# Decayed linear attention and a mixture of experts: state kept per whole block of 128 tokens instead of per half block

## The chip, the cores and the metric

The kernel runs on one core of a Trainium2 chip. A core has five engines that run their own instruction streams and meet through semaphores: TensorE (PE in the rows; PEld is its loading of weights), VectorE (DVE), ScalarE (ACT), GpSimd (POOL) and SyncE (SP), which here issues nearly all transfers. The metric is the time of one execution on the device in microseconds (us), less is better. An x in a row is a count.

## What is computed

```python
def _attn_ref(q, k, v, alpha):          # (4, 8, 768, 48) each
    state = np.zeros((B, H, D, D))
    for t in range(S):
        state = alpha[:, :, t, :, None] * state + np.einsum('bhd,bhe->bhde', k[:, :, t], v[:, :, t])
        y[:, :, t] = np.einsum('bhd,bhde->bhe', q[:, :, t], state)

def _moe_ref(x, w_skip, w_gate, w1, w2):  # x: (3072, 384), 8 experts, F = 1024
    do_compute = x @ w_skip > 0
    xc = x[do_compute]; logits = xc @ w_gate; e_idx = argmax(logits)
    gate_w = softmax(logits)[e_idx]
    h = relu(xc[e_idx == e] @ w1[e]);  y = gate_w * (h @ w2[e])
    out[do_compute] = xc + y              # the other rows stay x
```

## The kernel before, in words

The sequence of each batch is cut into six chunks of 128 tokens. Two batches are worked alternately, so there are 24 tiles (i = 0 to 23), each with all eight heads of 128 tokens; heads stand in four pairs p, the two heads of a pair on partitions 0 to 47 and 64 to 111 (r = 0, 1). A loop in `static_path` (line 829) runs one step per tile. The instructions of a step are written by hand for several tiles at once, and each engine runs them in the order in which that loop writes them, so the order of the calls is the schedule.

What the calls do for tile i:

- `load` (201): the transfers of decay factors, keys and queries (one tile `qka`) and of the values (`vt`), issued by SyncE five tiles ahead.
- `decay` part 0 and 1 (211): VectorE's running products from the front (`pfx`, 216) and from the back (`sfx`, 224); GpSimd multiplies the queries (220) and keys (226) by them.
- `scores` (229) and `causal` (240): keys times queries for each half of the block (64 keys by 64 queries) into `ps_s`, which VectorE then copies under the causal mask into `st`.
- `turn_k` (244): the keys transposed on TensorE, copied by ScalarE into `kt`.
- `outer` (256): keys times values, added into the state in PSUM (`ps_v`), once per half; after the first half ScalarE copies the half-way state (`half`, 272). `carry` (274) multiplies the state by the decay of the block on VectorE, and `keep` (280) copies it into `state` on ScalarE.
- `inter` (295): queries times state, the first 64 queries with `state`, the other 64 with `half`. `intra` (306): masked scores times values, in two calls. All of it adds up in `ps_y`; `turn_y` (327, its copy is line 330) takes it to SBUF as `xt`.
- `rows` (333), `row_copy` (343), `logits` (348), `store` (353): the output rows and the nine gate logits. `rows` writes into the same PSUM tile `ps_s` as the scores, and the scores of the next tile wait until VectorE has read the logits.

Beside this the loop routes finished tiles in groups of six: `rank` and `place` find slots, `one_hot` (421, line 424 in the rows, GpSimd) builds a 128 by 256 matrix for each tile, and `table` (431, line 436) multiplies with it on TensorE. For the first two groups two one-hot matrices are built per step in three steps (i = 10 to 12 and 16 to 18) and `table` uses them one step later. The weights of the first expert are loaded and split during the loop too. After the loop a tail routes the last tiles, and then eight experts follow (`up` 590, `down` 612).

## Time and profile before

| | |
|---|---|
| median of three runs | 323.0 us (322.78 to 326.44) |
| the profiled execution | 324.42 us, of it the span of the trace 322.6 us |
| busy share of the span | PE 85%, DVE 59%, POOL 59%, ACT 48% |
| TensorE instructions | 4920 matmuls, 4920 weight loads |
| granted TensorE clock, mean | 0.901 of full speed |
| stages in the trace | attention loop to about 158 us, tail to 168.5 us, experts to the end |

Times in the rows of the trace count from the start of the span. The granted clock has two levels, 1.2 and 2.4 GHz; 1.00 in a stretch means 2.4 GHz throughout, 0.50 means 1.2 GHz throughout. A matmul row that says 64*48 64x64 uses 64 rows and 48 columns of the array; TensorE runs several such small ones side by side. In single precision every matmul of the source is two instructions on TensorE, a transpose one. "issue" as a releaser means that an engine waited for nothing that the profile shows.

### The profile page before, as it was taken

How to read it: one execution, taken by the hardware profiler on the slowest of the kernel's cores; microseconds unless marked ns; L12 is line 12 of the kernel's file. 1: busy time of each engine (PE TensorE's matmuls, PEld its weight loads, DVE VectorE, ACT ScalarE, POOL GpSimd, SP SyncE). 2: the span in 40 equal slices, each digit the busy share in tenths (PEclk: the TensorE clock that was granted, in tenths of full speed). 3: DMA queues.
4: the chain of work that ended last, by engine and by line, in shares of the span. 5: the costliest groups of instructions: out<-in, count | busy, mean ns of one | idle time of the engine just before them, and what ended most of it. 6: DMA issues, size and time to landing. Idle time of an engine off the chain costs nothing.

```text
span 322.6 us, 11454 instructions
## 1 busy us (share of the span) xinstructions
PE 273.5 (85%) x4920; PEld 256.9 (80%) x4920; DVE 189.7 (59%) x367; ACT 153.5 (48%) x318; POOL 189.3 (59%) x208
## 2 busy tenths in 40 slices
PE   1997777876888788859789699999999799999991
PEld 1786766866777687759689599999999799999991
DVE  6877677475667566745446516547293576466640
ACT  3145334243335243443415636878685976455510
POOL 4555744445767458672794856737567476755521
PEclk9999799598768779795589689999999999999998
DMA  7997686676657657743502269349498599742000
GB/s 258 410 329 244 213 287 218 194 217 243 208 188 242 208 178 214 225 154 100 203 26 73 80 176 309 106 166 401 139 335 279 185 395 346 261 161 79 15 18 28
DMA packets 25850, 65.44 MB, mean 203 GB/s; under 512 B 3765, under 2 KB 10831, under 8 KB 25792
## 3 DMA queue, kind: packets, MB, share of 16 engines
q1 hardware_dynamic: 23616, 59.58, 55.1%
q0 software_dynamic: 2176, 5.05, 4.7%
q8 instruction: 40, 0.66, 0.8%
q14 instruction: 18, 0.15, 0.1%
HBM read 56.99 MB, written 8.85 MB: 204 GB/s over the span
## 4 chain that ended last, share of the span: by engine, by line
PE 54%; issue 11%; DMA 10%; DVE 8%; ACT 7%; POOL 7%; SPq 1%; POOLq 0%; DVEq 0%; ACTq 0%
PE ps_o L619 14%; PE ps_h L603 13%; PE ps_y L292 7%; PE ps_s L340 5%; DMA raw<-in_w_dram 4%; PE ps_v L266 4%; PE ps_s L237 3%; ACT over L572 3%; PE ps_k L250 3%; POOL hot L424 3%; DVE sfx L224 3%; DMA alpha<-in_nat_dram 3%; ACT x L345 2%; DMA qka<-in_qka_dram 2%; PE ps_g L436 2%
## 5 line engine op out<-in xcount | busy, mean ns | idle before, releaser
L226 POOL TENSOR_TENSOR qka<-qka,sfx 128x512 f32<-128x512 f32 x23 | 29.4, 1277 | 32.2 <-DVE sfx L224 29.2
L619 PE MATMUL ps_o<-w2h,hh 128*112 128x384 f32 (+1 forms) x128 | 44.7, 349 | 0.0
L619 PE MATMUL ps_o<-w2l,hh 128*112 128x384 f32 (+1 forms) x128 | 44.0, 344 | 0.0
L619 PE MATMUL ps_o<-w2h,hl 128*112 128x384 f32 (+1 forms) x128 | 43.7, 341 | 0.0
L220 POOL TENSOR_TENSOR qka<-qka,pfx 128x512 f32<-128x512 f32 x24 | 26.3, 1094 | 23.9 <-PE ps_k L250 8.4
L266 PE MATMUL ps_v<-vt,kt 64*64 64x48 f32 x704 | 36.1, 250 | 4.7 <-issue 4.0
L292 PE MATMUL ps_y<-st,vt 64*48 64x64 f32 x768 | 36.1, 257 | 3.9 <-issue 3.9
L252 ACT COPY kt<-ps_k 128x512 f32<-128x512 f32 x24 | 14.1, 586 | 53.1 <-PE ps_k L250 53.1
L539 POOL TENSOR_TENSOR w2l<-raw,w2h 128x512 fp32r<-128x512 f32 x18 | 24.3, 1351 | 24.6 <-ACT w2h L535 24.6
L266 PEld LDWEIGHTS ps_v<-vt,kt 64*64 64x64 f32 x704 | 32.3, 168 | 5.7 <-issue 4.6
L603 PE MATMUL ps_h<-xh,w1h 128*128 128x240 f32 x192 | 32.8, 277 | 4.0 <-DVE hl L608 2.8
L539 POOL TENSOR_TENSOR w1l<-raw,w1h 128x512 fp32r<-128x512 f32 x24 | 31.6, 1318 | 6.8 <-ACT w1h L535 6.6
L608 DVE SCALAR_TENSOR_TENSOR hl<-ps_h,hh 128x480 fp32r<-128x480 f32 x32 | 20.8, 650 | 22.3 <-ACT hh L607 22.2
L624 POOL DMA_INDIRECT out_dram<-o,ids x16 | 19.0, 1186 | 24.1 <-DVE o L622 23.0
L607 ACT ACTIVATE hh<-ps_h 128x480 fp32r<-128x480 f32 x32 | 18.3, 571 | 31.0 <-PE ps_h L603 27.0
L603 PE MATMUL ps_h<-xh,w1l 128*128 128x240 f32 x192 | 32.4, 275 | 0.0
L603 PE MATMUL ps_h<-xl,w1h 128*128 128x240 f32 x192 | 31.7, 274 | 0.0
L224 DVE TENSOR_TENSOR_SCAN sfx<-qka,ps_c 128x525 f32<-128x525 f32 x24 | 29.9, 1248 | 2.6 <-POOL qka L220 0.5
L216 DVE TENSOR_TENSOR_SCAN pfx<-qka,ps_c 128x527 f32<-128x527 f32 x24 | 29.8, 1241 | 2.6 <-DMA qka<-in_qka_dram 2.6
L292 PEld LDWEIGHTS ps_y<-st,vt 64*48 64x48 f32 x768 | 27.7, 146 | 4.4 <-issue 4.4
L237 PE MATMUL ps_s<-qka 64*64 64x64 f32 x768 | 23.0, 270 | 9.5 <-DVE qka L226 7.1
L603 PEld LDWEIGHTS ps_h<-xh,w1h 128*128 128x128 f32 x192 | 27.3, 190 | 4.6 <-DVE hl L608 3.1
(138 smaller groups left out, 628.3 us busy)
## 6 DMA issues: line engine op xcount, KB each, us to landing
raw<-in_w_dram SPq DMA_DIRECT2D x64, 384.0 KB, 5.4
qka<-in_qka_dram SPq DMA_DIRECT2D x22, 775.5 KB, 4.7
vt<-in_v_dram SPq DMA_DIRECT2D x24, 192.0 KB, 4.7
out_dram<-x SPq DMA_DIRECT2D x24, 192.0 KB, 2.6
alpha<-in_nat_dram SPq DMA_DIRECT2D x8, 576.0 KB, 4.1
out_dram<-xr SPq DMA_DIRECT2D x6, 192.0 KB
qka<-in_qka_dram SPq DMA_DIRECT2D x4, 256.0 KB
qka<-in_qka_dram SPq DMA_DIRECT2D x2, 263.5 KB
```

Source lines behind the costliest of these rows:

```text
L216: nc.vector.tensor_tensor_scan(pfx[:, 0:DEC], dec, self.floor.to_broadcast([P, DEC]), FLOOR, ALU.mult, ALU.max)
L220: nc.gpsimd.tensor_tensor(w["qh"], w["qh"], pfx.rearrange("p (a w) -> p a w", w=SEG)[:, :, 1:P + 1], ALU.mult)
L224: nc.vector.tensor_tensor_scan(sfx[:, 2:DEC][:, ::-1], dec[:, 2:DEC][:, ::-1], self.floor.to_broadcast([P, DEC - 2]), FLOOR, ALU.mult, ALU ...
L226: (eng or nc.gpsimd).tensor_tensor(w["kh"], w["kh"], sfx.rearrange("p (a w) -> p a w", w=SEG)[:, :, 2:P + 2], ALU.mult)
L237: self.nc.tensor.matmul(self.ps[t, r, p * HP:(p + 1) * HP], lhsT=kh[a, p, t], rhs=qh[a, p, t], start=True, stop=True, skip_group_check=True)
L266: ins = self.nc.tensor.matmul(pv[a, p, :], lhsT=w["kt"][t, p, a], rhs=w["v"][t, h * D:(h + 1) * D], start=(i % (G * C) == s == p == 0), st ...
L292: return self.nc.tensor.matmul(self.py[HP * c:HP * c + D, p % 2, o:o + HP], lhsT=lhsT, rhs=rhs, start=first, stop=True, skip_group_check=True)
L539: eng.tensor_tensor(lo[:, s], raw[:, s], hi[:, s].bitcast(F32), ALU.subtract)
L603: nc.tensor.matmul(ps[:, u, :], lhsT=a[:, k, f * P:(f + 1) * P], rhs=b[:, k, :], start=(n == 0), stop=(n == len(order) - 1))
L608: nc.vector.scalar_tensor_tensor(out=hl, in0=ps, scalar=0.0, in1=hh.bitcast(F32), op0=ALU.max, op1=ALU.subtract)
L619: nc.tensor.matmul(ps[:r], lhsT=a[:, f, js], rhs=b[:, f, :], start=(n == 0), stop=(n == 3 * FT - 1))
L624: ins = nc.gpsimd.indirect_dma_start(out=self.out[:, :], out_offset=bass.IndirectOffsetOnAxis(ap=self.ids[:r, j, e:e + 1].bitcast(U32), ax ...
```

## The change

In the loop, each tile's state is kept once per block of 128 tokens and no longer half-way. To make up for the missing half state, the scores of the first 64 keys are taken against all 128 queries (the other 64 keys still against their own 64 queries); the block between (first keys, last queries), which needs no mask, is copied by ScalarE in a new function `cross`. `inter` takes all 128 queries against the old state in one instruction, `outer` takes all 128 tokens at once, and `rows` takes both heads of a pair at once into a bank of its own (`ps_g`). The routing's small products move from `ps_g` into `ps_v`. The transfers of a tile are four instead of two, each issued behind a named matmul, six tiles ahead. One one-hot matrix is built per step in steps 10 to 21. The order of the step is new.

The core of the diff:

```diff
-RW = D + E + 1
+RW = 2 * D + E + 1
...
-    def load(self, i):
-        for s in (slice(0, DEC), slice(KO, QO), slice(QO, QW)) if i < NF else (slice(0, QW),):
-            nc.sync.dma_start(out=t[:, s], in_=self.qka[i, :, s])
-        nc.sync.dma_start(out=vt, in_=self.v[i])
+    def load(self, i, part=None, behind=None):
+        if part == 3:
+            ins = nc.sync.dma_start(out=self.work[i]["v"], in_=self.v[i])
+        else:
+            s = (slice(0, DEC), slice(KO, QO), slice(QO, QW))[part]
+            ins = nc.sync.dma_start(out=self.qkab[i % NQ][:, s], in_=self.qka[i, :, s])
+        if behind:
+            self.follow(ins.ins, behind)
...
     def scores(self, i):
-                    self.nc.tensor.matmul(self.ps[t, r, p * HP:(p + 1) * HP], lhsT=kh[a, p, t], rhs=qh[a, p, t],
-                                          start=True, stop=True, skip_group_check=True)
+                    o = p * P
+                    ins = self.nc.tensor.matmul(self.ps[t, r, o:o + (HP if s else P)], lhsT=kh[a, p, t],
+                                                rhs=qh[a, p, s * HP:], start=True, stop=True, skip_group_check=True)
...
+    def cross(self, i):
+        ps = self.ps.rearrange("k r (a q) -> k r a q", q=P)
+        self.nc.scalar.copy(out=self.work[i]["st"][:HP, :, :, HP:], in_=ps[:HP, :, :, HP:])
...
-    def outer(self, i, s):
+    def outer(self, i):
...
-                ins = self.nc.tensor.matmul(pv[a, p, :], lhsT=w["kt"][t, p, a], rhs=w["v"][t, h * D:(h + 1) * D],
-                                            start=(i % (G * C) == s == p == 0), stop=True, skip_group_check=True)
-        if s == 0:
-            self.nc.scalar.copy(out=w["half"], in_=pv)
+                self.nc.tensor.matmul(pv[a, p, :], lhsT=w["kt"][:, p, a], rhs=w["v"][:, h * D:(h + 1) * D],
+                                      start=(i % (G * C) == p == 0), stop=True, skip_group_check=True)
...
     def inter(self, i):
-        for s in range(2):
-            src = w["half"] if s else self.state[i % G]
-            for p in range(NP):
-                for r in range(2):
-                    self.product(i, p, r ^ p % 2, s, src[a, p, :], w["qh"][a, p, s * HP:(s + 1) * HP])
+        src = self.state[i % G]
+        for p in range(NP):
+            for r in range(2):
+                self.product(i, p, r ^ p % 2, 0, P, src[a, p, :], w["qh"][a, p, :])
...
     def intra(self, i, other):
-                ins = self.product(i, p, c, s, w["v"][t, h * D:(h + 1) * D], w["st"][t, r, p * HP:(p + 1) * HP])
+                n = HP if s else P
+                ins = self.product(i, p, c, s * HP, n, w["v"][t, h * D:(h + 1) * D], w["st"][t, r, p, 0:n])
...
     def rows(self, i):
-                for c in range(2):
-                    self.nc.tensor.matmul(self.ps[t, c, RO + p * RW:RO + (p + 1) * RW], lhsT=w["xt"][a, p, t],
-                                          rhs=self.xw[a, p, :], start=True, stop=True, skip_group_check=True)
+                ins = self.nc.tensor.matmul(self.pg[t, p * RW:(p + 1) * RW], lhsT=w["xt"][:PD, p, t],
+                                            rhs=self.xw[:PD, p, :], start=True, stop=True, skip_group_check=True)
...
             for i in range(NT):
+                self.decay(i + 3, 0)
+                    self.rows(i - 1)
+                    self.load(i + NQ, 0, self.work[i - 1]["rowed"])
+                    self.row_copy(i - 1)
+                self.outer(i)
+                self.turn_k(i + 2)
+                if 11 <= i < 22:
+                    self.table((i - 11,))
+                self.decay(i + 3, 1)
+                    self.logits(i - 1)
+                self.carry(i)
+                self.intra(i, 1)
+                self.load(i + NQ, 1, self.work[i]["before"])
+                self.turn_y(i)
+                self.scores(i + 2)
+                self.causal(i + 2)
+                self.cross(i + 2)
+                self.keep(i)
+                    self.load(i + NQ, 2, self.work[i + 2]["scored"])
+                self.inter(i + 1)
+                self.intra(i + 1, 0)
+                self.load(i + NQ, 3, self.work[i + 1]["before"])
-                if not last:
-                    self.scores(i + 1)
-                    self.causal(i + 1)
-                self.inter(i)
-                self.outer(i, 1)
-                self.carry(i)
-                if i + 3 < NT:
-                    self.decay(i + 3, 0)
-                self.intra(i, 0)
-                    self.turn_k(i + 2)
-                if i:
-                    self.rows(i - 1)
-                    self.row_copy(i - 1)
-                    self.logits(i - 1)
-                if i + 3 < NT:
-                    self.decay(i + 3, 1)
-                if not last:
-                    self.outer(i + 1, 0)
-                self.intra(i, 1)
-                self.turn_y(i)
-                self.keep(i)
...
+                if 10 <= i < 22:
+                    self.one_hot(i - 10, nc.gpsimd)
```

How the orders of the engines change, at three places of a plain step (the names are those of the tiles above, with the number of the buffer; the count at the end is of calls in the source).

TensorE, before: one step, from the scores of the tile in `qka_81` to the second call of `intra`.

```order
L237 MATMUL ps_s<-qka_81 64x64 x16
L292 MATMUL ps_y<-qka_86,state_105 48x64 x8
L292 MATMUL ps_y<-qka_86,half 48x64 x8
L266 MATMUL ps_v<-vt,kt 64x48 x8
L292 MATMUL ps_y<-st_103,vt 48x64 x8
L250 MATMUL ps_k<-ident,qka_82 128x128 x4
L340 MATMUL ps_s<-xw,xt_106 64x57 x16
L266 MATMUL ps_v<-vt,kt 64x48 x8
L292 MATMUL ps_y<-st_103,vt 48x64 x8
```

TensorE, of the change: the end of the first call of `intra`, then `rows`, `outer`, `turn_k` and the second call of `intra`; ahead of these rows stand the sixteen score matmuls, alternately two of 64x128 and two of 64x64, and eight of `inter` of 48x128.

```order
L308 MATMUL ps_y<-st_102,vt 48x64
L354 MATMUL ps_g<-xw,xt_107 64x105 x8
L288 MATMUL ps_v<-vt,kt 64x48 x8
L275 MATMUL ps_k<-ident,qka_85 128x128 x4
L308 MATMUL ps_y<-st_102,vt 48x64
L308 MATMUL ps_y<-st_102,vt 48x128
L308 MATMUL ps_y<-st_102,vt 48x64
L308 MATMUL ps_y<-st_102,vt 48x128
L308 MATMUL ps_y<-st_102,vt 48x64
L308 MATMUL ps_y<-st_102,vt 48x128
L308 MATMUL ps_y<-st_102,vt 48x64
L308 MATMUL ps_y<-st_102,vt 48x128
```

The step loses eight calls of `inter`, eight of `outer` and eight of `rows`, and the rest of the calls get wider; `rows` no longer stands between the writing of `ps_s` and its next use.

ScalarE, before: one step (keys, rows, half state, output, state).

```order
L252 COPY kt<-ps_k 128x512
L345 COPY x<-ps_s 128x2x4x48
L272 COPY half<-ps_v 128x192
L330 COPY xt_107<-ps_y 112x512
L284 COPY state_105<-ps_v 128x192
```

ScalarE, of the change: one step (rows, keys, output, the new copy, state).

```order
L360 COPY x<-ps_g 128x384
L277 COPY kt<-ps_k 128x512
L346 COPY xt_107<-ps_y 112x512
L267 COPY st_103<-ps_s 64x8x64
L300 COPY state_105<-ps_v 128x192
```

The copy of the half state is gone, and the new copy of the scores stands between the output and the copy of the state.

VectorE, before: logits, back product, masked scores, decay of the state, front product, reciprocal.

```order
L350 TENSOR_REDUCE ps_c<-ps_s 128x9
L224 SCALAR_TENSOR_TENSOR sfx<-qka_81,ps_c 128x525
L242 COPY_PREDICATED st_103<-mask,ps_s 128x512
L278 TENSOR_TENSOR ps_v<-ps_v,pfx 128x192
L216 SCALAR_TENSOR_TENSOR pfx<-qka_82,ps_c 128x527
L218 RECIPROCAL qka_82<-pfx 128x4
```

VectorE, of the change: the same six, the logits after both products.

```order
L228 SCALAR_TENSOR_TENSOR pfx<-qka_82,ps_c 128x527
L230 RECIPROCAL qka_82<-pfx 128x4
L236 SCALAR_TENSOR_TENSOR sfx<-qka_82,ps_c 128x525
L367 TENSOR_REDUCE ps_c<-ps_g 128x9
L295 TENSOR_TENSOR ps_v<-ps_v,pfx 128x192
L261 COPY_PREDICATED st_102<-mask,ps_s 128x8x64
```

Both long products now stand in a row behind the masked copy, and the logits behind them.

## Rows read from the trace of the kernel before

**Rows 1.** Stretches: engines' busy us (instructions), granted clock, DMA share, GB/s.

```profile
20.00:60.00 40.00, 31.34 (x1166) 27.14 (x1163) 29.15 (x53) 15.78 (x39) 20.55 (x34) 0.93 0.76 240
20.00:140.00 120.00, 96.19 (x3171) 85.00 (x3169) 80.23 (x158) 46.64 (x110) 70.97 (x94) 0.84 0.69 221
```

**Rows 2.** Time order on ScalarE, line 330 only: start us, duration us, what.

```profile
22.11 0.59 ACT L330 COPY xt<-ps_y 112x512 f32<-112x512 f32 x1
...
27.47 0.59 ACT L330 COPY xt<-ps_y 112x512 f32<-112x512 f32 x1 [0.44 <-PE ps_y L292]
...
31.88 0.59 ACT L330 COPY xt<-ps_y 112x512 f32<-112x512 f32 x1
...
53.92 0.59 ACT L330 COPY xt<-ps_y 112x512 f32<-112x512 f32 x1
...
62.34 0.59 ACT L330 COPY xt<-ps_y 112x512 f32<-112x512 f32 x1
...
72.41 0.59 ACT L330 COPY xt<-ps_y 112x512 f32<-112x512 f32 x1
...
94.25 0.59 ACT L330 COPY xt<-ps_y 112x512 f32<-112x512 f32 x1 [0.19 <-PE ps_y L292]
...
146.10 0.59 ACT L330 COPY xt<-ps_y 112x512 f32<-112x512 f32 x1
```

**Rows 3.** Time order on TensorE: two waits named issue.

```profile
57.28 0.26 PE L292 MATMUL ps_y<-qka,half 64*48 64x64 f32 x2 [2.07 <-issue]
...
108.47 0.42 PE L266 MATMUL ps_v<-vt,kt 64*64 64x48 f32 x7 [2.36 <-issue]
```

**Rows 4.** Stretches as in Rows 1, for the counts of TensorE.

```profile
0.00:57.20 57.20, 40.70 (x1365) 35.41 (x1365) 41.79 (x69) 21.53 (x49) 30.54 (x50) 0.97 0.81 278
0.00:67.35 67.35, 50.03 (x1619) 43.92 (x1619) 48.00 (x82) 25.25 (x58) 34.73 (x57) 0.92 0.80 269
0.00:108.40 108.40, 81.70 (x2636) 71.91 (x2637) 73.75 (x134) 40.57 (x93) 60.97 (x87) 0.89 0.76 251
```

**Rows 5.** Waits: waiter, releaser, us in total, times, longest.

```profile
PE ps_y L292 <- issue: 5.9, 5, 2.1
...
PE ps_v L266 <- issue: 4.0, 3, 2.4
...
PE ps_g L436 <- POOL hot L424: 5.4, 11, 0.7
```

**Rows 6.** Groups by line and shape on VectorE, then ScalarE: busy us, mean ns.

```profile
L224 DVE TENSOR_TENSOR_SCAN sfx<-qka,ps_c 128x525 f32<-128x525 f32 x24 | 29.9, 1248 | 2.6 <-POOL qka L220 0.5
...
L216 DVE TENSOR_TENSOR_SCAN pfx<-qka,ps_c 128x527 f32<-128x527 f32 x24 | 29.8, 1241 | 2.6 <-DMA qka<-in_qka_dram 2.6
...
L242 DVE COPY_PREDICATED st<-mask,ps_s 128x512 f32<-128x512 uint8 x24 | 17.4, 724 | 1.4 <-PE ps_s L237 1.4
...
L278 DVE TENSOR_TENSOR ps_v<-ps_v,pfx 128x192 f32<-128x192 f32 x20 | 7.3, 365 | 12.6 <-PE ps_v L266 12.6
...
L252 ACT COPY kt<-ps_k 128x512 f32<-128x512 f32 x24 | 14.1, 586 | 53.1 <-PE ps_k L250 53.1
...
L284 ACT COPY state<-ps_v 128x192 f32<-128x192 f32 x20 | 6.5, 324 | 0.0
```

**Rows 7.** Time order on TensorE: warm, half-clock, and full-array instructions.

```profile
22.76 0.44 PE L292 MATMUL ps_y<-qka,state 64*48 64x64 f32 x16
...
23.02 0.40 PE L292 MATMUL ps_y<-qka,half 64*48 64x64 f32 x16
...
147.12 0.65 PE L292 MATMUL ps_y<-qka,state 64*48 64x64 f32 x16
...
147.55 0.65 PE L292 MATMUL ps_y<-qka,half 64*48 64x64 f32 x16
...
164.02 0.39 PE L494 MATMUL ps_v<-ident,xr 128*128 128x128 f32 x2
...
164.24 0.39 PE L494 MATMUL ps_y<-ident,xr 128*128 128x128 f32 x2
```

More of the change, by code (lines that the diff above doesn't have):

```diff
@@ L122, in attention_pools @@
         self.hp = st.enter_context(tc.tile_pool(name="hp", bufs=7))
-        self.stb = [fix.tile([P, 2, NP * HP], F32, name=f"st{i}") for i in range(2)]
+        self.stb = [fix.tile([P, 2, NP, P], F32, name=f"st{i}") for i in range(2)]
         self.state = [fix.tile([P, NP, D], F32, name=f"state{b}") for b in range(G)]
@@ L138, in early_constants @@
         make_identity(nc, self.ident)
+        self.spot = const.tile([1, 1], F32, name="spot")
         self.ones = const.tile([P, P], F32, name="ones_f")
@@ L184, in slot_constants @@
         self.lim = const.tile([P, 2], F32, name="lim")
-        self.spot = const.tile([1, 1], F32, name="spot")
         nc.gpsimd.memset(self.lim[:, 0:1], A_MIN)
@@ L277, in carry @@
         pv = self.region[i % G]
-        ins = self.nc.vector.tensor_tensor(pv, pv, self.work[i]["total"].to_broadcast([P, NP, D]), ALU.mult)
-        self.carried = ins.ins.name
+        self.nc.vector.tensor_tensor(pv, pv, self.work[i]["total"].to_broadcast([P, NP, D]), ALU.mult)
     def keep(self, i):
@@ L432, in table @@
     def table(self, tiles, tb=None):
-        tb = self.pg[:, GO:GO + NB * MW] if tb is None else tb
+        start = tb is not None
+        tb = self.pv[:, TO:TO + NB * MW] if tb is None else tb
         for j in range(NB):
@@ L814, in static_path @@
             self.early_constants()
-            for i in range(1, 6):
+            for i in range(1, NQ):
                 self.load(i)
@@ L897, in static_path @@
                         self.one_hot(t, nc.vector)
+                if i == 11:
+                    self.table_add(first=True)
                 if i == 22:
```

161 lines of the change are left out of this document (84 added, 77 removed).

## The prediction

> **What bounds the kernel now.** I read the stretches first. Between 20 and 140 us, the attention loop, no engine is full: TensorE is busy 96 of 120 us, VectorE 80, GpSimd 71, ScalarE 47, and the granted clock is 0.84 [rows 1]. With two levels, 1.2 and 2.4 GHz, a mean of 0.84 means that 32% of the time passed at the lower one. So the loop is a chain of waits, and I next read its beat. One instruction per step is easy to follow, ScalarE's copy of line 330 [rows 2]. It starts at 22.11 for tile 1 and at 146.10 for tile 21: 20 steps in 124.0 us, 6.20 us each. The beat is uneven. A good step takes 4.41 us (27.47 to 31.88). Another takes 8.42 (53.92 to 62.34), and the three from 72.41 to 94.25 take 7.28 each. The question is what makes 4.4 into 7 or 8.
>
> For the long single steps, the time order of TensorE shows waits named issue, 2.07 and 2.36 us long [rows 3]: nothing in the program held the engine. The counts tell what they are. When the two begin, 1365 and 2636 matmuls have run, and 1619 at 67.35, where a third one begins [rows 4]: 254 and 1017 apart, two and eight times 127. Each matmul has its weight load, so 127 are 254 instructions. I read these waits as the fetching of instructions in blocks of a fixed size: there are 3171 matmuls from 20 to 140 us [rows 1], hence some 25 blocks, and two lines of the waits alone hold 9.9 us in 8 waits [rows 5]. The Trainium skill (Runtime: NRT & Kernel Launch, Instruction fetch mechanics) says that instructions are refilled in blocks of 256 and that crossing a block's edge is mostly hidden. The trace agrees on the size and not on the hiding. By that rule these 9.9 us have another cause and stay, which is weighed below as a rival.
>
> For the three steps after 72.41, the waits name GpSimd's one-hot matrices: TensorE waits 11 times, 5.4 us in total, for two of them per step [rows 5]. After such waits, and after those named issue, the clock falls: 0.93 up to 60 us, 0.84 over all [rows 1].
>
> The good step is set by VectorE. Its four long instructions per tile are 1.25, 1.24, 0.72 and 0.37 us, 3.58 in sum [rows 6]; with the logits, a reciprocal and the gaps between them that comes near 4.41. Over the stretch VectorE is busy 80.2 us in 19.4 steps, 4.1 us each, since the routing adds to it.
>
> **The change part by part.**
>
> *TensorE's work.* Small matmuls run side by side here. Warm, sixteen instructions of 64 columns start from 22.76 to 23.02, 16 ns each; at half the clock from 147.12 to 147.55, 27 ns each [rows 7]. A pair with the whole array and 128 columns takes 0.22 us (164.02 to 164.24), 110 ns each. A quarter of the array for half the columns should then take an eighth of 110, 14 ns, and takes 16: the array's streaming sets the pace, since halving the clock nearly doubles it. At 0.86 ns for a column of the whole array, the new step costs: scores 8 instructions of 128 columns in each of two quarters, 0.88 us; inter 16 of 128 in four quarters, 0.44; the two calls of intra 0.44 each, set by the quarters with 128 columns; rows 16 of 105 columns, two at a time, 0.72; outer 16 at 64 columns of weights, two at a time, 0.44; transposes 4 of 128, 0.44. In sum 3.8 us warm and, times 27/16 to 2, 6.4 to 7.6 us at half the clock; I take 7.2. The same counting gives 2.8 us for the old step. So the change removes 24 calls, 48 of 164 instructions per step, and still gives TensorE about 1 us more to stream. The other bound is that only the number counts: 116 instructions at 16 ns are 1.9 us. I take the upper one, because the two clocks show streaming.
>
> *The chain of a step.* The new ScalarE copy waits for VectorE's masked copy, the copy of the state stands behind it, and TensorE's outer waits for that. Behind outer wait the transposes, intra and the next scores. This loop is: masked copy 0.72, new copy at most 0.59 (the row of a 128x512 copy; half the partitions, as many elements each; if it cost nothing, the loop would be that much shorter), state 0.32 [rows 6], then outer 0.44, transposes 0.44, intra 0.44, scores 0.88, and about 0.5 for the matmuls' drain and the handing over (the matmul rows last 0.4 us for a pair that starts every 0.22). That is 4.3 us. VectorE's round is 4.1 busy and some 0.4 of gaps, 4.5. Both meet, so I take 4.6 us for an undisturbed step; the gain lies in the disturbed ones. VectorE's own work is unchanged, and its logits, put behind both products, no longer wait for ScalarE's copy, nor do the scores wait for the logits.
>
> *One-hot matrices.* One per step, used a step later with 5 us between: the waits of 5.4 us go. GpSimd does the same sum of work.
>
> *Fetches and transfers.* 116 of 164 instructions means 71% of the blocks, 18 in place of 25. The 9.9 us become 7.0 for that reason alone. A tile's keys, queries and decay, 128 x 1551 floats or 794 KB in one burst before, go in three pieces of a third, each behind a named matmul. If the wait goes with the burst, a third of 7.0 is left, 2.3. I take the middle, 4.7 us. SyncE issues in order, so behind each piece that waits for TensorE stand the next pieces, the stores and the weights. They are needed three steps later, or five steps for the stores, and this costs nothing as long as a piece lands within some 13 us.
>
> *Clock.* The falls come after long waits, and most of these go; TensorE's share rises as well. I take 20% of the time at the lower level in place of 32%. A mean step is then 1/(0.8/4.6 + 0.2/7.2) = 4.95 us.
>
> *The rest.* Before 22 us and after 146 us the same work runs: the first tiles wait for transfers and a cold array, the tail for routing. The experts are TensorE's own from there on. I take both as moved, not changed.
>
> *Sum.* 20 steps at 4.95 are 99.0, with 4.7 of fetching 103.7 in place of 124.0: 20.3 us less. Against the profiled execution's own 324.4 us that is 304.1. The median of the runs is 1.4 lower, so the forecast on that scale is **302.7 us**.
>
> **The rivals.**
>
> *The clock and the waits stay (still faster).* If fetching is not what the issue waits are, as the page's rule would have it, 9.9 us stay, and if the clock stays at 32% low, a step is 1/(0.68/4.6 + 0.32/7.2) = 5.20 us. 20 x 5.20 + 9.9 = 113.9: 10 us less, 313. For it speaks that the count of waits is short; against it, that the waits stand whole multiples of 127 matmuls apart.
>
> *Streaming doesn't matter.* With 1.9 us per step TensorE is never the bound, cold or warm. 20 x 4.6 + 2.3 = 94: 30 us less, 293. The pace at two clocks speaks against it.
>
> *Transfers become the bound (no change).* From 20 to 60 us the transfer engines are busy 76% at 240 GB/s [rows 1]; full would be 316 GB/s. These 9.6 MB in 7.0 steps of 5.75 us (22.11 to 62.34) are 1.38 MB per step, 4.4 us when full. At 5.2 us per step the share would be 0.84, close enough that each fetch could queue. With 1.2 us for each of the 18 blocks (half the longest wait), 99 + 21.6 = 120.6: 320 us. Smaller pieces and six tiles of lead speak against it.
>
> *TensorE cold (slower).* Its place is the loop, its price 7.2 us for a cold step against 4.6. It decides when the cold share passes 63%: there 1/(0.37/4.6 + 0.63/7.2) is 5.96, which with 0.24 of fetching per step is the old 6.20. At 80% a step is 6.47 + 0.24 = 6.7, 10 us more: 333. For it speaks that a cold step is now longer and that chains of waits on ScalarE are added; against it, that a cold TensorE would be busy without a break, and that the clock came back each time before (0.93 in a stretch that holds the wait at 57.28).
>
> **How the numbers follow.** Forecast (between 298 and 309) 0.50, waits and clock stay 0.18, streaming doesn't matter 0.12, transfers 0.12, cold 0.08. The range from 292 to 318 takes in the first three. A difference of 2% (6.5 us) is about what a measurement of this kernel can tell from no change. The first three are faster by more than that: 0.80. The transfers' case is within it, with a little of the second: 0.12. Slower is 0.08.
>
> **What would show it.** Right: line 346, which takes the place of 330, starts every 4.6 to 5.2 us; TensorE has about 3,800 matmuls; the wait of line 455 on the one-hot matrices is gone; waits named issue in the loop sum to 3 to 7 us and are each under 1.5; the granted clock from 20 us to the loop's end is 0.88 or more; scores of a warm step start-to-end about 0.9 us; the experts take as long as before. Wrong: the clock under 0.7 with TensorE full (cold), a transfer share above 0.9 with waits of VectorE on `qka` (transfers), or outer waiting over 0.5 us in each step for ScalarE's copy of the state, which would make the loop longer than the 4.6 us that I reckon.

## The result, and the profile after

The changed kernel takes **300.9 us** in the median of four runs (300.43 to 301.84), where the kernel before took 322.9 beside it (319.45 to 326.44). The ratio is 0.9355, with a 95% interval from 0.9277 to 0.9433. The forecast was 302.7, its range 292 to 318. Some executions of a kernel fall into a slower state, over 1.5% above its fastest: medians and ranges here take in all runs, ratios and their intervals only the others.

The profiled execution has a span of 298.8 us in place of 322.6. I cut it at ScalarE's copy of a tile's products (line 346 now, 330 before). The copy of tile 1 starts at 25.33 us where it started at 22.11: the part ahead of the loop became 3.2 us longer. The 20 steps to the copy of tile 21 took 96.1 us in place of 124.0: 27.9 less. The last two steps took 1.4 less, and what follows them 2.3 more. In sum 23.8 us less. So the forecast's total was near, but the loop gained more than was forecast, and both ends, which were to stay, gave 5.5 us back. The 2.3 us stand in the experts, whose first matmul starts 10.6 us behind the last copy in both kernels: they last 156.4 us in place of 154.1, at a granted clock of 0.95 in place of 0.97. In the kernels below that did not change them either (experiment 5 apart) they last 153.3 to 157.0 us, so this difference lies within their scatter.

The beat, on ScalarE in order of time (start us, duration us, what), to be read against [rows 2]:

```profile
25.33 0.59 ACT L346 COPY xt<-ps_y 112x512 f32<-112x512 f32 x1
29.88 0.59 ACT L346 COPY xt<-ps_y 112x512 f32<-112x512 f32 x1
34.36 0.58 ACT L346 COPY xt<-ps_y 112x512 f32<-112x512 f32 x1
38.85 0.58 ACT L346 COPY xt<-ps_y 112x512 f32<-112x512 f32 x1
...
85.24 0.59 ACT L346 COPY xt<-ps_y 112x512 f32<-112x512 f32 x1 [0.21 <-PE ps_y L308]
90.88 0.58 ACT L346 COPY xt<-ps_y 112x512 f32<-112x512 f32 x1 [0.33 <-PE ps_y L308]
96.54 0.58 ACT L346 COPY xt<-ps_y 112x512 f32<-112x512 f32 x1 [0.20 <-PE ps_y L308]
...
121.42 0.58 ACT L346 COPY xt<-ps_y 112x512 f32<-112x512 f32 x1
```

The early steps are even, 4.5 us each (4.48 for most). The steps of 7 and 8 us are gone. The longest are now 5.6 (85.24 to 90.88, 90.88 to 96.54), in the places where a group of tiles is routed.

The stretches, as in [rows 1] (busy us and instructions of TensorE, its weight loads, VectorE, ScalarE and GpSimd; granted clock, DMA share, GB/s). The changed kernel's 20 steps end at 121.42 us, so the stretch to 120 us is set beside the same stretch of the kernel before, which is the last line:

```profile
20.00:60.00 40.00, 39.19 (x1006) 33.56 (x998) 32.19 (x57) 21.26 (x46) 23.65 (x37) 0.98 0.84 258
20.00:120.00 100.00, 94.02 (x2367) 81.27 (x2359) 82.06 (x160) 53.98 (x118) 72.64 (x95) 0.99 0.87 277
```

```profile
20.00:120.00 100.00, 80.29 (x2669) 70.97 (x2667) 65.79 (x126) 38.98 (x92) 56.19 (x74) 0.84 0.70 225
```

The page's line on instruction transfers (packets, MB, share), which had 40 packets before:

```profile
q8 instruction: 31, 0.51, 0.7%
```

TensorE is busy 94 of 100 us, with fewer instructions, where it was busy 80. The granted clock is 0.99, where it was 0.84. The waits say why it is no longer idle (waiter, releaser, us in total, times, longest); TensorE has none named issue, and its wait for the one-hot matrix, 5.4 us in [rows 5], is down to 0.3:

```profile
DVE st L261 <- PE ps_s L252: 10.4, 13, 2.1
...
PE ps_v L288 <- DVE ps_v L433: 2.0, 2, 1.0
...
PE ps_v L288 <- ACT state L300: 1.2, 4, 0.5
...
PE ps_v L455 <- POOL hot L442: 0.3, 1, 0.3
```

One undisturbed step in order of time. Lines: 252 scores, 308 inter and intra, 354 rows, 288 outer, 275 transposes; 261 VectorE's masked copy, 267 the new ScalarE copy, 300 the copy of the state:

```profile
42.85 0.32 PE L252 MATMUL ps_s<-qka 64*64 64x128 f32 x2
...
42.97 1.13 PE L252 MATMUL ps_s<-qka 64*64 64x64 f32 x30
...
43.97 0.66 PE L308 MATMUL ps_y<-qka,state 64*48 64x128 f32 x16
44.19 0.73 DVE L261 COPY_PREDICATED st<-mask,ps_s 128x512 f32<-128x512 uint8 x1 [0.48 <-PE ps_s L252]
...
44.45 0.61 PE L308 MATMUL ps_y<-st,vt 64*48 64x128 f32 x16
...
44.99 0.95 PE L354 MATMUL ps_g<-xw,xt 112*64 112x105 f32 x16
45.01 0.58 ACT L267 COPY st<-ps_s 64x512 f32<-64x512 f32 x1 [1.09 <-DVE st L261]
45.49 0.31 ACT L300 COPY state<-ps_v 128x192 f32<-128x192 f32 x1
...
45.86 0.67 PE L288 MATMUL ps_v<-vt,kt 128*64 128x48 f32 x16
...
46.46 0.66 PE L275 MATMUL ps_k<-ident,qka 128*128 128x128 f32 x4
...
47.05 0.55 PE L308 MATMUL ps_y<-st,vt 64*48 64x64 f32 x14
47.33 0.32 PE L252 MATMUL ps_s<-qka 64*64 64x128 f32 x2
```

From scores to scores (42.85 to 47.33) are 4.48 us, and TensorE shows hardly a gap. Yet outer starts at 45.86, just behind the end of the state's copy (45.49 and 0.31 are 45.80). So two readings stand side by side: TensorE's own stream closes the loop, or the chain masked copy, new copy, state, outer does. And for the loop as a whole there are two more: the issue waits went because there are fewer instructions, or because a tile comes in pieces. The experiments take these apart.

### The profile page after: what moved, and what is told of

Same layout as the page of the kernel before. It is cut to its first block, busy times and chain, and to the rows that moved or that the text cites. A ratio compares the mean times of both kernels' runs of the same rounds, so it can differ in the third digit from the quotient of the medians.

```text
span 298.8 us, 9251 instructions
## 1 busy us (share of the span) xinstructions
PE 264.2 (88%) x3768; PEld 245.9 (82%) x3768; DVE 192.5 (64%) x368; ACT 157.9 (53%) x317; POOL 188.4 (63%) x208
## 4 chain that ended last, share of the span: by engine, by line
PE 45%; DMA 16%; DVE 14%; ACT 8%; POOL 7%; issue 6%; SPq 2%; POOLq 0%; DVEq 0%; ACTq 0%
PE ps_o L637 15%; PE ps_h L621 13%; DMA raw<-in_w_dram 9%; ACT over L590 5%; PE ps_y L308 5%; DMA alpha<-in_nat_dram 4%; PE ps_s L252 4%; DVE sfx L236 3%; DVE pfx L228 3%; DVE st L261 3%; PE ps_k L275 2%; PE ps_v L288 2%; POOL hot L442 2%; PE ps_g L354 2%; DMA qka<-in_qka_dram 2%
## 5 line engine op out<-in xcount | busy, mean ns | idle before, releaser
L252 PE MATMUL ps_s<-qka 64*64 64x128 f32 (+1 forms) x768 | 31.5, 264 | 7.6 <-DVE qka L238 7.6
L308 PE MATMUL ps_y<-st,vt 64*48 64x64 f32 (+1 forms) x768 | 31.7, 253 | 3.1 <-ACT x L360 1.9
L621 PE MATMUL ps_h<-xl,w1h 128*128 128x240 f32 x192 | 32.3, 278 | 0.0
L640 DVE SCALAR_TENSOR_TENSOR o<-ps_o,gates,xr 128x384 f32<-128x384 f32 (+1 forms) x16 | 9.9, 616 | 34.6 <-PE ps_o L637 34.6
L252 PEld LDWEIGHTS ps_s<-qka 64*64 64x64 f32 x768 | 25.7, 139 | 7.8 <-POOL st L153 7.6
L553 ACT CAST w1h<-raw 128x512 fp32r<-128x512 f32 x48 | 27.6, 621 | 5.8 <-DMA raw<-in_w_dram 5.8
L267 ACT COPY st<-ps_s 64x512 f32<-64x512 f32 x24 | 13.9, 579 | 29.4 <-DVE st L261 26.1
```

Of the source, the lines that this page charges most:

```text
L252: ins = self.nc.tensor.matmul(self.ps[t, r, o:o + (HP if s else P)], lhsT=kh[a, p, t], rhs=qh[a, p, s * HP:], start=True, stop=True, skip_ ...
L308: return self.nc.tensor.matmul(self.py[HP * c:HP * c + D, p % 2, o:o + n], lhsT=lhsT, rhs=rhs, start=first, stop=True, skip_group_check=True)
L553: nc.scalar.copy(out=hi[:, s], in_=raw[:, s])
L621: nc.tensor.matmul(ps[:, u, :], lhsT=a[:, k, f * P:(f + 1) * P], rhs=b[:, k, :], start=(n == 0), stop=(n == len(order) - 1))
```

## The experiments

Each run also left a profile. Times are medians, ratios those to the kernel before on the same chip; the loop is the 20 steps from tile 1's copy to tile 21's, 96.1 us in the changed kernel and 124.0 before. Waits named issue are counted up to the last tile, two steps further. The expectations call some runs by their labels: e3_split is experiment 3, e7_keep experiment 6, e6_prologue and e10_route the two edits of experiment 8, e11_both the first of experiment 9.

**1. One transfer per tile again.** The pieces undone, nothing else:

```diff
 def load(self, i, part=None, behind=None):
...
-            s = (slice(0, DEC), slice(KO, QO), slice(QO, QW))[part]
+            s = (slice(0, QW), slice(KO, QO), slice(QO, QW))[part]
+            if i < NQ:
+                s = (slice(0, DEC), slice(KO, QO), slice(QO, QW))[part]
+            elif part:
+                return
```

> The changed kernel with a tile's decay, keys and queries in one transfer of 794 KB again (from tile 6 on), put behind the same matmul as the first piece was; nothing else differs, so TensorE has its 3768 matmuls. Theory 'bursts' (a fetch of instructions is late when it stands behind a whole tile's burst): TensorE's waits named issue come back in the loop, 8 or 9 of some 1 us (71% of the 12 of before), the granted clock of the loop falls from 0.99 to about 0.9, and the time is 306 to 312 us. Theory 'count' (they are gone because there are fewer instructions): no such wait in the loop, clock 0.97 or more, 300 to 302 us.

Measured: 302.7 us (300.02 to 306.79), ratio 0.937 (0.923 to 0.952). TensorE has two waits named issue, 0.4 us each, one of them behind the 20 steps. The loop is 98.7 us; part of the 2.6 us more lies in a stretch from 72 to 76 us with a granted clock of 0.71. 'Bursts' is refuted: 794 KB in one piece bring next to none of the 12.9 us of before back (9.9 of them stand in [rows 5]). 'Count', which said none and 300 to 302 us, is nearer. Cutting the transfers was worth nothing that these runs can tell.

**2. The kernel before with its transfers in pieces.** The mirror image; `piece` issues one part of a tile behind the named matmul:

```diff
 self.causal(i + 1)
+self.piece(i + 5, 0, self.work[i + 1]["scored"])
 tick(2)
 self.inter(i)
+self.piece(i + 5, 1, self.work[i]["inner"])
 self.intra(i, 0)
+self.piece(i + 5, 2, self.work[i]["before"])
 self.intra(i, 1)
+self.piece(i + 5, 3, self.work[i]["before"])
```

> The kernel before, where from tile 6 on a tile's decay, keys and queries go in three pieces, each behind a named matmul of the step (scores, inter, first call of intra), and the values behind the second call of intra. TensorE's instructions and their order are those of before. Theory 'bursts': the waits named issue in the loop fall from some 12 us to under 4, the clock rises from 0.84 to 0.9 or more, and the time is 306 to 316 us. Theory 'count': 10 or more such waits stay, the clock stays at 0.84, and the time is 320 to 325 us.

Measured: 324.1 us (320.65 to 327.88), ratio 1.008 (1.001 to 1.015). The waits of TensorE:

```profile
PE ps_v L282 <- issue: 5.5, 3, 2.7
PE ps_y L308 <- issue: 4.3, 5, 1.6
...
PE ps_s L252 <- issue: 3.1, 3, 1.6
```

With 0.5 us in one more they are 12 waits and 13.4 us; the kernel before has 12 and 12.9. The clock is 0.86 from 20 to 140 us. 'Bursts' falls a second time; the time is the one that 'count' gave.

**3. The old number of calls, with the new columns.** In the changed kernel each matmul of 128 columns becomes two of 64, so a step has 164 matmul instructions again in place of 116. Shown is the product of inter and intra; scores are cut likewise:

```diff
-return self.nc.tensor.matmul(self.py[HP * c:HP * c + D, p % 2, o:o + n], lhsT=lhsT, rhs=rhs, start=first,
-                             stop=True, skip_group_check=True)
+for u in range(0, n, HP):
+    ins = self.nc.tensor.matmul(self.py[HP * c:HP * c + D, p % 2, o + u:o + u + HP], lhsT=lhsT,
+                                rhs=rhs[:, u:u + HP], start=first and u == 0, stop=True, skip_group_check=True)
...
+return ins
```

> The changed kernel with each matmul of 128 columns in scores, inter and intra cut into two of 64 columns: 24 calls more in a step, about as many as before the change, the same columns in all. Transfers in three pieces as they are. Theory 'columns set TensorE's pace, bursts set the fetch': the steady step stays within 0.1 us of 4.48, no issue waits, 300 to 303 us. Theory 'the count of instructions sets the pace and the fetch': issue waits come back (up to 12 us) or the step gets longer by 48 instructions at 16 ns, 0.77 us in 20 steps, and the time is 310 to 320 us.

Measured: 321.9 us (318.52 to 323.76), the time of before and more than the 310 to 320 of 'count'. The loop takes 115.5 us, 19.4 more than in the changed kernel. The waits of TensorE, then two of them in order of time, then the counts of matmuls up to there:

```profile
PE ps_y L311 <- issue: 6.7, 5, 2.2
PE ps_v L290 <- issue: 4.8, 2, 2.8
PE ps_g L359 <- issue: 3.4, 3, 2.4
...
PE ps_s L254 <- issue: 0.7, 2, 0.4
```

```profile
36.73 0.32 PE L290 MATMUL ps_v<-vt,kt 128*64 128x48 f32 x2 [1.94 <-issue]
...
58.34 0.48 PE L359 MATMUL ps_g<-xw,xt 112*64 112x105 f32 x5 [2.37 <-issue]
```

```profile
0.00:36.70 36.70, 23.16 (x602) 20.14 (x602) 24.23 (x35) 12.54 (x26) 17.86 (x29) 0.95 0.80 253
0.00:58.30 58.30, 41.96 (x1238) 36.80 (x1238) 39.56 (x60) 21.84 (x45) 28.89 (x46) 0.97 0.80 250
```

Twelve waits are back, 15.6 us (eleven of them, 14.6 us, within the 20 steps), though the transfers still come in pieces. The two shown stand at 602 and 1238 matmuls, 636 apart, which is five times 127 within one record, as in [rows 4]; all eleven of the loop stand whole multiples of 127 apart, each within one record of the one before. Undisturbed steps take 4.75 us, 0.27 more than 4.48. Over 20 steps that is 5.4 us; the other 14 of the 19.4 are about what the waits come to. So the number of instructions carries most of the gain of this change: 19.4 of the 27.9 us of the loop.

**4. Many instructions, but slowly.** Is it each block that costs, or the pace at which blocks are used up? To the kernel of experiment 3, four wide matmuls per step are added (and the part of `ps_y` that they write is cleared at the start):

```diff
 self.inter(i + 1)
+for p in (0, 1):
+    for b in (0, 1):
+        nc.tensor.matmul(self.py[:, b, 2 * P:], lhsT=self.ident,
+                         rhs=self.work[i + 1]["kh"][:, 2 * p:2 * p + 2, :].rearrange("p a t -> p (a t)"),
+                         start=False, stop=True, skip_group_check=True)
 self.intra(i + 1, 0)
```

> The kernel e3_split (as many small matmuls as before the change, 164 matmul instructions per step) with four matmuls of 128x256 columns more per step, whose result nobody reads: 8 instructions more, but some 1.75 us of streaming (four times two halves of 0.22). A block of 127 matmuls then lasts at least some 4.8 us, in place of 3.7 in e3_split's undisturbed step of 4.75 us and 4.9 in the changed kernel's of 4.48. Theory 'rate' (the fetch takes about 4.5 us per block and keeps up when TensorE takes longer over a block): the waits named issue, 15.6 us in e3_split, fall to under 3 us although there are more instructions; steps of some 6.5 us, 338 to 346 us. Theory 'count' (each block that is crossed costs its share): 14 us or more of such waits stay, 352 to 362 us.

Measured: 344.0 us, steps of 6.6 us for the most part. TensorE has more instructions than in any kernel so far (5040 matmuls), and this is its only wait named issue:

```profile
PE ps_y L311 <- issue: 0.6, 1, 0.6
```

'Rate' is right. The load of the transfer engines does not explain the waits: from 20 to 60 us they are busy 0.72 of the time in experiment 3, 0.57 here and 0.84 in the changed kernel, which has no such wait either. A block of 127 matmuls lasts 6.6 x 127/172 = 4.9 us there, and the next one is ready. In experiment 3 an undisturbed step asks for a block each 4.75 x 127/164 = 3.7 us, and TensorE stands. With the waits it got one each 5.77 x 127/164 = 4.5 us on average. The changed kernel asks for one each 4.48 x 127/116 = 4.9 us and has none. Of the kernels that follow, those that ask for one each 4.9 us have no wait in the loop or two (up to 1.7 us in all), and the three that ask for one each 4.7 us, in experiments 5 and 6 and the last of experiment 9, have two or three (1.4 to 1.9 us). The limit is not sharp; it lies between 4.5 and 4.9 us per block. Four of these kernels (experiment 6, the second edit of 8, the first and third of 9) have a wait at 73 to 78 us, right behind one to three short steps of about 4.0 us, in which a block lasts 4.4 us or less; the changed kernel has one such step and no wait.

**5. Fewer columns in intra.** Its first 64 keys meet 64 queries in place of 128:

```diff
 def intra(self, i, other):
-    n = HP if s else P
+    n = HP
```

> The changed kernel without the products of a tile's first 64 keys with its last 64 queries in intra (the matmuls keep their number and take 64 columns in place of 128; that contribution is left out of the output). The new ScalarE copy stays. By the running pace both calls of intra fall from some 0.44 to 0.22 us. Theory 'TensorE's stream sets the steady step': the step falls from 4.48 to some 4.1 us, where VectorE's busy time takes over; 293 to 296 us. Theory 'VectorE or the chain of masked copy, new copy and state sets it': the step stays at 4.4 to 4.5 and the time within 2 us of 300.9.

With these products left out the program also ran its general path (`general_attention`, `general_experts`), 6044 us in all, presumably since the routing comes out otherwise. So only the attention loop is read. Undisturbed steps take 4.27 us, 0.21 less; predicted by the one theory were 4.1, by the other 4.4 or more. The loop is 94.7 us. Neither expectation holds. Both calls of intra got narrower, but only one lies between outer and the end of the next scores; the other runs beside VectorE's masked copy. From outer's start to the next masked copy are 2.60 us in place of 2.81. One call's worth of 0.2 us is what a chain through outer would give back.

**6. The state ahead of the new copy.** ScalarE's order alone:

```diff
 self.causal(i + 2)
-self.cross(i + 2)
 self.keep(i)
+self.cross(i + 2)
```

> The changed kernel with ScalarE's copy of the state ahead of the copy of the products between; nothing else moves. The state is then copied behind the carry, without VectorE's masked copy and the 0.58 us of the other copy in between. Theory 'chain' (masked copy, copy between, state, outer close the loop of a step, 4.3 us by the prediction's sum): the undisturbed step falls from 4.48 to 4.1 or less. Theory 'TensorE's own stream closes it': it stays at 4.45 to 4.5 us, and the 20 steps at 95 to 97 us.

Measured: 300.1 us in one run; undisturbed steps of 4.33 us, the loop 93.5. The step in order of time:

```profile
39.60 0.32 ACT L300 COPY state<-ps_v 128x192 f32<-128x192 f32 x1
...
39.85 0.74 DVE L261 COPY_PREDICATED st<-mask,ps_s 128x512 f32<-128x512 uint8 x1 [0.33 <-PE ps_s L252]
...
40.65 0.95 PE L354 MATMUL ps_g<-xw,xt 112*64 112x105 f32 x16
...
41.42 0.62 PE L288 MATMUL ps_v<-vt,kt 128*64 128x48 f32 x16
```

The state is copied 1.5 us before outer, rows take 0.77 us to outer's start in place of 0.87, and no matmul of the step shows a wait. So the chain did close the changed kernel's step, and by 0.15 us only: behind it TensorE's own stream of 4.33 us comes next, and VectorE, which still waits 0.33 us for the scores, is not the bound. 'Chain' was right on the mechanism, wrong on the 4.1.

**7. Two one-hot matrices per step again.** The table uses them likewise, a step later:

```diff
-if 10 <= i < 22:
-    self.one_hot(i - 10, nc.gpsimd)
+for g0 in (0, 6):
+    if g0 + 10 <= i < g0 + 13:
+        n = g0 + 2 * (i - g0 - 10)
+        for t in (n, n + 1):
+            self.one_hot(t, nc.gpsimd)
```

> The changed kernel with two one-hot matrices per step in steps 10 to 12 and 16 to 18 again, used two at a time a step later, as before the change; all else as changed. Theory 'the spreading pays by itself': TensorE's waits for GpSimd's one-hot matrix, 0.3 us in the changed kernel, come back with some 5 us, and the time is 304 to 306 us. Theory 'with five microseconds and a whole step between they are hidden either way': waits under 1.5 us and 300 to 302 us.

Measured: 303.5 us (301.28 to 306.71), between the two, and the ratio, 0.9355 (0.925 to 0.946), is that of the changed kernel. TensorE waits for them twice, both at the start of the first group:

```profile
71.14 0.28 PE L455 MATMUL ps_v<-mv,hot 128*128 128x32 f32 x1 [0.26 <-POOL hot L442]
72.05 0.51 PE L455 MATMUL ps_v<-mv,hot 128*128 128x32 f32 x3 [0.62 <-POOL hot L442]
```

Then the clock falls, in a stretch (columns as above) in which the changed kernel has full clock and more matmuls. First this kernel, then the changed one:

```profile
74.00:78.00 4.00, 4.00 (x70) 3.56 (x64) 2.74 (x5) 1.07 (x3) 4.00 (x5) 0.72 0.72 192
```

```profile
74.00:78.00 4.00, 4.00 (x104) 3.65 (x100) 3.69 (x9) 2.08 (x5) 4.00 (x5) 1.00 0.93 294
```

The waits are 0.9 us, not 5. So most of the 5.4 us go with the new order alone, without the spreading. The loop is 3.3 us longer, 2.8 of it in the steps to tiles 11 and 12. But the kernel of experiment 1, which builds no pairs and waits 0.3 us for a one-hot matrix like the changed kernel, loses its clock at the same place, and its step to tile 12 takes 5.24 us in place of 4.02 (5.60 here):

```profile
72.00:76.00 4.00, 3.64 (x67) 3.23 (x65) 2.53 (x4) 2.40 (x5) 3.62 (x5) 0.71 0.99 357
```

So the fall of the clock cannot be put down to the pairs, and what they cost beyond the 0.9 us of waits is not shown.

**8. VectorE's order before the loop, and where the routing stands.** Two edits, each alone:

```diff
 self.decay(1, 0)
+self.decay(1, 1)
 self.causal(0)
 self.cross(0)
-self.decay(1, 1)
...
 self.decay(2, 0)
+self.decay(2, 1)
 self.causal(1)
 self.cross(1)
-self.decay(2, 1)
```

> The changed kernel with VectorE's order before the loop put back: the suffix scans of tiles 1 and 2 ahead of the masked copies of tiles 0 and 1. Nothing else moves. The ScalarE copy of tile 1's products now starts at 25.33 us, before the change at 22.11. Theory 'that order costs the 3 us': it starts at 22 to 23.5 us and the time is 298 to 299.5 us. Theory 'the cold scores or the transfers of the first tiles cost them': it stays at 25 us and the time at 300 to 302 us.

```diff
 self.decay(i + 3, 0)
+for g in groups[:3]:
+    if i == g[1] + (3 if g[0] == 12 else 4):
+        for _ in self.place(g):
+            pass
...
     tick(99)
-    for _ in self.place(g):
-        pass
...
-tick({19: 11, 21: 6, 22: 99}.get(i, 2))
+tick({7: 3, 13: 3, 19: 3, 21: 6, 22: 99}.get(i, 2))
```

> The changed kernel with VectorE's routing moved within its order: the place of a group's slots (three instructions) half a step later, behind the next prefix scan, and ScalarE's exponential one group of routing instructions earlier, so that VectorE's sum no longer stands right behind it. No work added or removed. Steps 15 and 16 now take 5.64 and 5.66 us, 19 to 21 about 5.4 to 5.6, against 4.48. Theory 'VectorE's waits for ScalarE (1.06 and 0.92 us) and TensorE's for the cleared slots (0.97) make these steps long': they fall to some 4.8 us and the time to 297 to 299 us. Theory 'the routing's own VectorE work does': they stay over 5.3 and the time is 300 to 302 us.

The first gave 298.2 us (295.68 to 298.74). Tile 1's copy starts at 23.63 us, just above the 22 to 23.5 expected, so 1.7 of the 3.2 us come back. The intervals of the ratios overlap (0.9125 to 0.9317 here), but the traces agree: six other kernels with the changed order start this copy at 25.67 to 26.80 us (the slowed one of experiment 4 at 28.27), and of the three more with the order put back, in experiment 9, two start it at 23.30 and 23.58 (the third at 26.00, with a granted clock of 0.55 to 0.59 from 20 to 28 us). What the changed kernel's order does is seen in its own trace:

```profile
14.87 0.73 DVE L261 COPY_PREDICATED st<-mask,ps_s 128x512 f32<-128x512 uint8 x1 [1.91 <-PE ps_s L252]
15.49 1.23 DVE L236 TENSOR_TENSOR_SCAN sfx<-qka,ps_c 128x525 f32<-128x525 f32 x1
...
16.80 1.27 POOL L238 TENSOR_TENSOR qka<-qka,sfx 128x512 f32<-128x512 f32 x1 [2.80 <-DVE sfx L236]
...
18.12 1.11 PE L275 MATMUL ps_k<-ident,qka 128*128 128x128 f32 x4 [2.83 <-POOL qka L238]
```

The masked copy waits 1.91 us for scores, tile 2's suffix scan stands behind it, GpSimd waits for that, and the transposes for GpSimd. After this wait the granted clock is 0.50 from 18 to 21 us; with the order put back it is 1.00 there. The other 1.5 us were not traced to a cause.

The second gave 299.1 us (298.37 to 301.47), between its two theories. The steps where the exponential stood got shorter (5.64 to 5.20 for tile 15, 5.38 to 4.73 for tile 20), the step of the place itself did not (5.66 to 5.96 for tile 16, 5.63 to 6.00 for tile 21). There outer waits, 1.27 us where it was 0.97 in the changed kernel:

```profile
94.99 0.10 DVE L433 MEMSET ps_v<- 128x48 f32 x1
```

```profile
95.23 0.67 PE L288 MATMUL ps_v<-vt,kt 128*64 128x48 f32 x16 [1.27 <-DVE ps_v L433]
```

The slots and the states share one bank of PSUM but no column. Outer waits all the same, about 1.0 us of it after the copy of the state, its releaser in other steps, had ended at 94.18. The chain of a step has the same form: the copy of the state for which outer waits reads the columns of one batch, and outer adds into those of the other. A bank for each batch was not tried. The Trainium skill (PSUM — Partial Sum Buffer, Terms) says that the compiler's back end keeps engines apart per bank and quadrant; this wait agrees, though no run here tells that rule from another reason for the order.

**9. Put together.** The first with both edits, and with the place between the carry and the masked copy, so that the slots are cleared before the state's copy; the second with rows in whole tiles on top; the third the first with the state ahead of the new copy:

```diff
 self.carry(i)
+for g in groups[:3]:
+    if i == g[1] + (2 if g[0] == 12 else 3):
+        for _ in self.place(g):
+            pass
 self.intra(i, 1)
```

> A version meant to be faster: the changed kernel with VectorE's order before the loop put back (as in e6_prologue), the exponential one group of routing instructions earlier (as in e10_route), and a group's place right behind the carry and ahead of the masked copy, where e10_route had it behind the prefix scan. There outer stood waiting 1.27 us for the cleared slots; here they are cleared before the copy of the state that outer waits for anyway. If gains add up: 2.6 us of the first, 1 to 3 of the others, 294 to 297 us, and no wait of outer for the cleared slots. If the waits only move to the masked copy's followers: 297 to 299 us.

```diff
-for s in range(2):
-    t = slice(HP * s, HP * (s + 1))
-    ins = self.nc.tensor.matmul(self.pg[t, p * RW:(p + 1) * RW], lhsT=w["xt"][:PD, p, t],
-                                rhs=self.xw[:PD, p, :], start=True, stop=True, skip_group_check=True)
+ins = self.nc.tensor.matmul(self.pg[:, p * RW:(p + 1) * RW], lhsT=w["xt"][:PD, p, :],
+                            rhs=self.xw[:PD, p, :], start=True, stop=True, skip_group_check=True)
```

> e11_both with rows in whole tiles: 4 calls of 128 tokens in place of 8 of 64, so 8 matmul instructions fewer per step, and on the whole array the same columns: 8 instructions of 105 at 0.86 ns are 0.72 us, while 16 in halves were measured at 0.87 from their first start to outer's. Theory 'rows in halves cost something (weight loads in halves)': the undisturbed step falls by 0.1 to 0.2 us, 2 to 4 us less than e11_both. Theory 'whole weight loads hide worse': the step grows by 0.1 us or more. If only the columns count: within 1 us of e11_both.

```diff
-self.cross(i + 2)
 self.keep(i)
+self.cross(i + 2)
```

> e11_both with the copy of the state ahead of the copy between, as in e7_keep. In e7_keep the undisturbed step fell from 4.48 to 4.33 us and the 20 steps from 96.1 to 93.5; in e11_both the 20 steps were 94.15 and the time 295.8. If the two add up: undisturbed steps of 4.33 us, 20 steps in 91 to 92.5 us and 293 to 295 us. If what e11_both moved had already taken the same waits: steps of 4.33 but 20 steps still over 93, and 295 to 297 us.

The first took 295.8 us (295.37 to 297.79), ratio 0.9195 (0.9126 to 0.9263). Outer's wait for the cleared slots, 2.0 us, is gone; its waits for the copy of the state grew from 1.2 to 2.1 us. By the medians the gains add up, and the time lies in the 294 to 297 expected.

The second took 299.3 (296.03 to 302.69), 3.5 more, with undisturbed steps of 4.68 us in place of 4.48 and a loop of 96.2 us in place of 94.2. From rows' start to outer's are 1.07 us, with half as many instructions:

```profile
37.68 1.14 PE L352 MATMUL ps_g<-xw,xt 112*128 112x105 f32 x8
38.75 0.67 PE L288 MATMUL ps_v<-vt,kt 128*64 128x48 f32 x16
```

So rows in halves, whose shape I had given no price, are worth 0.2 us per undisturbed step, as the theory of whole weight loads had it. Why is open; the columns alone do not explain it, as they are the same. The weight loads are a candidate that no run tests: eight whole ones last 0.97 us in the trace, sixteen halves 0.74. In the time the difference is not certain: the intervals of the two ratios overlap (0.917 to 0.936 here), and of the 3.6 us between the profiled executions 2.4 lie ahead of the loop, at the low clock named in experiment 8.

The third took **293.2 us** (292.46 to 295.33), ratio 0.914 (0.908 to 0.920), the fastest here: 7.6 us below the changed kernel by the medians; the intervals of the two ratios do not overlap. Its undisturbed steps take 4.34 us and its loop 92.9, between the two expectations. Its block then lasts 4.75 us, and the fetch is late again in two places:

```profile
PE ps_s L252 <- issue: 1.7, 1, 1.7
...
PE ps_y L308 <- issue: 0.2, 1, 0.2
```

## Why the prediction was right, and where it was not

*What bounds the kernel now* held in the main: the loop was a chain with waits of several kinds, and the change moved them. The fetch in blocks of 127 matmuls held most of all, with the waits of experiment 3 again whole multiples apart. "The good step is set by VectorE" did not: in the step from 27.47 to 31.88 VectorE stands 0.33 us for outer and 0.57 us for ScalarE's copy of the rows. Over the 20 steps it waited 28.4 us for that copy ahead of the logits, and 0.8 in the changed kernel, where `rows` has a bank of its own and the logits stand behind both products; what this part is worth by itself no run tests.

*Fetches* had the right cause and the wrong size. The step that failed is the sentence "71% of the blocks, 18 in place of 25. The 9.9 us become 7.0 for that reason alone", with a further cut for smaller transfers, to 4.7 us. Measured: none. It treated each block as costing its share. It also started from 9.9 us in two lines of the waits, where all lines hold 12.9 in 12 waits. It is a rate: below some 4.5 to 4.9 us per block the fetch is late, above it costs next to nothing (experiment 4), and size or time of the other transfers does not matter (experiments 1 and 2). The rule of the Trainium skill (Runtime: NRT & Kernel Launch, Instruction fetch mechanics), that crossing a block's edge is mostly hidden, is right by these runs where a block lasts 4.9 us and wrong at 3.7.

*TensorE's work* was counted too low: 3.8 us per step, measured 4.33 in experiment 6, where nothing else is waited for. Scores take 1.1 us in place of 0.88, transposes 0.59 for 0.44, outer 0.60 for 0.44, rows 0.87 for 0.72. That columns rather than the count set the warm pace held within a step: 48 instructions more at equal columns cost 0.27 us (experiment 3), where 16 ns each would be 0.77. But the count set the loop's time through the fetch, which is why "streaming doesn't matter" was nearer in its loop, 94 us, than in its reason.

*The chain of a step* was right: 4.3 us by the sum, 4.48 measured, and experiments 5 and 6 show that it closes the loop. The new copy takes 0.58 us, the bound that was taken. From outer's start to the next masked copy are 2.81 us, where the sum had 2.7 with all of its 0.5 for draining and handing over. VectorE's round, put at 4.5, is not the bound: it still waits 0.48 us per step for scores. So the undisturbed step is 4.48 in place of the 4.6 taken.

*Clock* was right in its direction and much too careful. I took 20% of the loop at the lower level; the granted clock is 1.00 in every stretch of four microseconds from 24 to 124 us, so none of the 20 steps ran at the lower one. Whether long waits pull it down, as I argued, is not settled: experiment 3 has 15.6 us of waits named issue and a clock of 0.95 from 20 to 140 us, experiment 2 has 13.4 and 0.86.

*One-hot matrices*: the wait went, as said, but not for the reason given. In the new order the pairs wait 0.9 us in all, so the spreading was worth at most 0.6 us of waits, not 5.4 (experiment 7).

*The rest* failed: "the same work runs" before 22 us and after 146. Ahead of the loop, 3.2 us longer, the new order of VectorE puts the suffix scans behind a wait for scores; 1.7 us come back when the order is put back. The 2.3 us behind the loop stand in the experts and lie within their scatter, 153.3 to 157.0 us from kernel to kernel.

*Sum.* Forecast for the loop: 20 x 4.95 + 4.7 = 103.7. Measured: 96.1, or 20 x 4.48 = 89.6 and 6.5 us in the routing steps, which had no term of their own. The loop gained 7.6 us more than forecast, the ends lost 4.1 (3.2 - 1.4 + 2.3) that were not forecast. Against the profiled execution's 304.1 the forecast is thus 3.5 us too long, and 1.8 on the scale of the medians. That it came so near is partly luck: a fetching term of 4.7 us that did not come and a clock that was taken too low were offset by the routing steps and by losses at the ends, which I had not forecast.

Of the loop's 27.9 us the runs attribute 19.4 to the number of instructions. The other 8.5 hold the one-hot matrices, the clock, the logits that no longer wait for the rows' copy, and the shifted chain; how they share them stays open. Of the rivals, *Transfers become the bound* did not come true: the transfer engines are busy 0.87 from 20 to 120 us, and VectorE has no wait for `qka` in the loop.

## What to carry to other kernels

Where a trace shows TensorE waiting for nothing in the program, count matmuls between such waits: equal multiples mean that the instruction fetch is late, and then fewer, wider matmuls help, while reshaping the data transfers does not. Reckon it as a rate, instructions per microsecond in the shortest steps, since here a kernel below the limit paid next to nothing and one above it paid in stalls; a further speed-up of the step brings the stalls back. After such a change look at the work that was "only moved": here 3 us were lost ahead of the loop, and a copy put in front of a more urgent one cost 0.15 us in every step.

## What the runs showed of the hardware

- The fetch supplies TensorE with some 127 matmuls (and their weight loads) per 4.5 to 4.9 us. A tile's 794 KB in one burst beside it brought two waits, 0.8 us in all (experiment 1).
- Rows on the whole array (8 instructions of 105 columns) took 1.07 us, on two halves (16 instructions) 0.87, and 0.77 where outer had no copy to wait for (experiments 9 and 6).
- Outer stood 1.27 us until a memset of other columns of its PSUM bank was done, about 1.0 of it for that alone (experiment 8).
